# Gated recurrent attention and a PReLU network in one kernel: three edits of a hand-written order

## The chip, the cores and the metric

The kernel runs on one core of a Trainium2 chip. A core has five engines that each work through their own list of instructions in order: TensorE (PE in the profile, with its weight loads as PEld), VectorE (DVE), ScalarE (ACT), GpSimd (POOL) and SyncE (SP), which only issues transfers. ScalarE and POOL issue transfers too. The engines meet through semaphores alone. The metric is the device time of one execution in microseconds (us), lower is better.

## The reference

A recurrence per batch and head (4 batches, 8 heads, 768 steps in time, 48 dimensions), followed by a two-layer network on its output:

```python
f = 1.0 / (1.0 + np.exp(-f_logit))
for t in range(S):
    state = f[:, :, t, :, None] * state + np.einsum('bhd,bhe->bhde', k[:, :, t], v[:, :, t])
    y[:, :, t] = np.einsum('bhd,bhde->bhe', q[:, :, t], state)
x = y.transpose(0, 2, 1, 3).reshape(B * S, H * D)        # 3072 x 384
h = x @ w_in                                             # 384 x 2048
g = np.maximum(h, 0.0) + alpha * np.minimum(h, 0.0)
return g @ w_out                                         # 2048 x 384
```

## The kernel before, in words

Time is cut into 6 chunks of 128, the batches into 2 pairs. A step is one chunk of one pair, so there are 12 steps, and each handles 256 tokens. Inside a chunk the recurrence is unrolled into products of decayed q and k over blocks of 32 and 64, with a state carried from chunk to chunk in the v tile `vs`.

The work of a step is written as four generators, which give control back at every `yield`:

- `prepare` loads f, q, k and v, takes the sigmoid, and builds the decays and the scaled q and k, nearly all on VectorE. Its last part copies `q3` into `A` on ScalarE (L407).
- `carry` multiplies across blocks (`off`, L432 and L442), copies that into `ad` and `A` on ScalarE (L446, L450), in the first chunk also transposes k on TensorE (`pk`) and copies it (`ksn`, L462). A second part makes the state's update (`pd`) and adds it to `vs` (L482 to L488).
- `attend` makes the products inside the blocks of 32 (`raw` L508, `qu` L523), places them under masks on VectorE (L514, then L529 or L545), copies them into `A` (L551), multiplies with `vs` (`py`, L562) and copies the result to `y`. `y` becomes `xT`: in the first step by products with a 0/1 matrix (`xt`, L580), later by small transfers (L591).
- `network` computes the two layers for the step's 256 tokens: `ph` (L606) into a PSUM bank, its negative part on ScalarE (`neg`, L611), the gate on VectorE (L613). In the first step the second layer is the plain product `po` (L626). From the second on it is seven products of half matrices (`pa` to `pe`, L645), which need sums of gates (`S`, L687) and sums of quarters of w_out (t2, t3, t4 and b12, L706).

The weights come as 64-bit floats and are turned into 32-bit ones on the chip, in 8 pieces each for w_in and w_out. A piece is one load on SP's queue (L196) into one of 4 `raw` buffers, three ScalarE activations (L201, L203, L204, some 2.6 us together), and then on VectorE a difference (L214, `lead`) and a 16-bit addition (L219). SP's load of a piece waits until the third activation of the piece four before it has read the buffer. Piece n of w_in serves the n-th `ph` of the first step; piece n of w_out serves two of the 16 row blocks of `po`.

PSUM is shared out in two pools that go round: two pairs of banks (`off`, `pk`, `raw`, `qu`, `pd`, `py`) and four single banks (`xt`, `ph`, `po`, `pa` to `pe`). A product that takes a bank waits until the reader of the tile before has finished with it. So the first `po` takes the bank that the gates of the fifth `ph` free, and in later steps the first `ph` takes the bank of `pb`, which L668 frees.

Nothing plans the order on TensorE, VectorE and ScalarE. It is written out by hand in strings, one per step, and the instructions of these three engines are issued in exactly the order in which the strings call the generators (POOL and SP follow from what the tiles need). Each letter advances one generator to its next `yield`, and a digit repeats it:

- `P` is the step's own `prepare`, `Q` the `prepare` of the step after it, `O` is `carry`, `S` is `attend`, and `n` is `network` of the step before.
- `a` is the ScalarE part of the next w_in piece and its load, `w` the VectorE part: the difference of one piece and the addition of the piece before it. `b` and `v` are the same for w_out.
- `W` advances `halves_of_w_out`: the first call only makes room, then come t3, t2, t4 and b12, each in two VectorE instructions.

The first four steps have strings of their own in `first` (L712 to L717), all others share `usual`.

Of the kernel before, what the change touches and what calls it, by code (L numbers as in the profile page):

```python
# [31 lines left out]
def kernel(  # L32
# [39 lines left out]
    W = U * HP * C  # L72
# [66 lines left out]
    for m in range(1, NB):  # L139
        lo = UO[m] + (4 if m == 1 else 0)  # L140
        n = NB - m
# [4 lines left out]
    for half in range(2):  # L146
        for m in range(1, NQ):
            n = NQ - m
# [540 lines left out]
    def halves_of_w_out():  # L689
# [20 lines left out]

    steps = [(bp, c) for c in range(NC) for bp in range(B // U)]
    first = (  # L712
        "P5 a w P a2 O w S w a w a2 S Q S O S w Q2 S Q2 S w",
        "a2 w b w n O w n b2 v S P v2 n2 S b v Q n b n O S2 v n b v n Q2 b v Q b n S v2 W Q W S n2 W n W",
        "n S P n2 S n W n O Q n3 O S Q n S Q n Q S2 Q n3",
        "S n3 P S Q S n O n O n4 Q S Q S Q n S Q n Q n2",
    )  # L717
    usual = "S n2 S n O n O n Q n3 Q n Q S3 n Q S n Q n Q n"
# [80 lines left out]
```

## Time and profile before

| | us |
|---|---|
| median of 3 runs | 623.29 |
| lowest and highest | 623.14, 623.50 |
| the profiled execution, whole | 625.07 |
| its span, first to last instruction | 623.3 |
| granted TensorE clock over the span | 0.997 |

An instruction row of the profile gives its start, its length (of several merged ones, from first start to last end), engine, line, operation, output and input, shape and count. In square brackets stand the idle time of the engine just before it and what ended it. A row of the chain or of waits names who waited for whom. Times of instructions overlap slightly, because an engine's next instruction starts before the last one has been written out.

The start-up (loads, weights, the first step) reaches to about 105 us, when the second step's first `ph` begins. From about 157 us on the kernel goes round once per step, in equal distances of 47.3 us, until about 534 us; behind that come the rest of the last step and the network of its tokens.

### The profile page before, as it was taken

The page shows a single profiled execution, that of the slowest core. Times are in us where ns is not written, and L with a number is a line of the kernel's source. Part 1 is how long each engine was busy: PE and PEld are TensorE (multiplying, and loading weights), DVE is VectorE, ACT ScalarE, POOL GpSimd, SP SyncE. Part 2 cuts the span into 40 slices and gives each one's busy share as a digit, 9 for nine tenths or more (in the row PEclk, how much of TensorE's full clock was granted, in tenths as well). Part 3 has the DMA queues.
Part 4 walks back from the last instruction along what each step waited for, and adds up shares of the span by engine and source line. Part 5 has one row for each costly group of instructions (what it writes and reads, how often), then busy time and mean ns, then how long its engine had stood idle before and what let it go on. Part 6 is the DMA issues. An engine that isn't in the chain of part 4 may idle for free.

```text
span 623.3 us, 19117 instructions
## 1 busy us (share of the span) xinstructions
PE 589.7 (95%) x8220; PEld 526.0 (84%) x8220; DVE 503.7 (81%) x1013; ACT 260.4 (42%) x482; POOL 62.7 (10%) x119
## 2 busy tenths in 40 slices
PE   3458999999999999999999999999999999999997
PEld 3347866789899899889889889889889889889997
DVE  7589989899799699899889888888888889762261
ACT  5797992270443252352342343343243244223110
POOL 9020010001001001001001001001001000000000
PEclk9999999899999999999999999999999999999999
DMA  9865613213313313313313413313313301201000
GB/s 306 271 226 187 215 40 90 72 35 88 85 36 93 79 35 86 87 35 85 88 35 85 87 36 85 87 35 87 73 49 85 71 19 26 53 3 26 26 1 25
DMA packets 68116, 50.43 MB, mean 81 GB/s; under 512 B 47168, under 2 KB 60608, under 8 KB 68032
## 3 DMA queue, kind: packets, MB, share of 16 engines
q1 hardware_dynamic: 56656, 25.01, 15.6%
q0 software_dynamic: 6864, 22.35, 12.3%
q10 hardware_dynamic: 4512, 1.85, 1.6%
q8 instruction: 65, 1.06, 0.7%
q14 instruction: 19, 0.16, 0.1%
HBM read 36.21 MB, written 4.72 MB: 66 GB/s over the span
## 4 chain that ended last, share of the span: by engine, by line
PE 58%; DVE 15%; ACT 12%; issue 3%; ACTq 0%; DMA 0%; DVEq 0%
PE ph L606 23%; PE pc L645 9%; PE pa L645 6%; PE pe L645 5%; PE pd L645 5%; ACT A L551 4%; DVE gate L613 3%; ACT us L302 3%; DVE S L687 3%; PE qu L523 3%; PE raw L508 2%; DVE qd L275 2%; PE py L562 2%; ACT neg L611 2%; PE pb L645 1%
## 5 line engine op out<-in xcount | busy, mean ns | idle before, releaser
L606 PE MATMUL ph<-xT,w_in_sb 128*128 128x256 f32 x1152 | 262.3, 385 | 0.0
L606 PEld LDWEIGHTS ph<-xT,w_in_sb 128*128 128x128 f32 x1152 | 216.4, 191 | 32.9 <-issue 2.5
L611 ACT ACTIVATE neg<-ph 128x512 f32<-128x512 f32 x96 | 57.2, 597 | 196.5 <-PE ph L606 157.3
L613 DVE SCALAR_TENSOR_TENSOR gate<-neg,om,ph 128x256 f32<-128x256 f32 x192 | 82.1, 477 | 48.9 <-ACT neg L611 48.7
L645 PE MATMUL pc<-t,S 128*128 128x192 f32 x352 | 61.7, 329 | 0.0
L645 PE MATMUL pa<-w_out_sb,gate 128*128 128x192 f32 x352 | 61.0, 327 | 0.0
L645 PEld LDWEIGHTS pa<-w_out_sb,gate 128*128 128x128 f32 x352 | 58.0, 190 | 0.6
L645 PEld LDWEIGHTS pc<-t,S 128*128 128x128 f32 x352 | 57.3, 190 | 0.6
L514 DVE COPY_PREDICATED ad<-mraw,raw 128x256 f32<-128x256 int32 (+1 forms) x96 | 42.4, 442 | 8.3 <-PE raw L508 5.8
L529 DVE COPY_PREDICATED ad<-mquad,qu 128x224 f32<-128x224 int32 (+6 forms) x140 | 42.0, 300 | 6.2
L407 ACT COPY A<-q 48x512 f32<-48x512 f32 x44 | 27.2, 617 | 37.5 <-DVE q L356 37.1
L551 ACT COPY A<-ad 32x256 f32<-32x256 f32 x96 | 38.6, 402 | 1.4
L318 DVE TENSOR_TENSOR us<-us,fs 128x768 f32<-128x768 f32 (+5 forms) x60 | 36.8, 614 | 0.0
L663 ACT COPY o<-pa 128x192 f32<-128x192 f32 x11 | 3.5, 319 | 75.2 <-PE pa L645 72.3
L508 PEld LDWEIGHTS raw<-qd,k 48*32 48x32 f32 x1536 | 18.4, 109 | 16.6 <-issue 8.8
L562 PEld LDWEIGHTS py<-A,vs 128*64 128x64 f32 x768 | 25.7, 145 | 7.8 <-ACT A L551 3.3
L508 PE MATMUL raw<-qd,k 48*32 48x80 f32 x1536 | 23.4, 243 | 9.3 <-ACT A L450 7.0
L562 PE MATMUL py<-A,vs 128*64 128x64 f32 x768 | 28.8, 232 | 3.4 <-ACT vs L488 1.3
L687 DVE TENSOR_TENSOR S<-gate 128x512 f32<-128x512 f32 x44 | 30.3, 688 | 0.8
L645 PE MATMUL pb<-t,gate 128*128 128x192 f32 x176 | 30.4, 326 | 0.0
L645 PE MATMUL pd<-w_out_sb,S 128*128 128x192 f32 x176 | 30.4, 326 | 0.0
L645 PE MATMUL pe<-w_out_sb,S 128*128 128x192 f32 x176 | 30.4, 326 | 0.0
(109 smaller groups left out, 756.0 us busy)
## 6 DMA issues: line engine op xcount, KB each, us to landing
w_out_raw<-in_w_out SPq DMA_DIRECT2D x8, 767.8 KB, 4.2
w_in_raw<-in_w_in SPq DMA_DIRECT2D x8, 767.2 KB, 9.9
q<-in_qT POOLq DMA_DIRECT2D x11, 512.0 KB, 4.1
f<-in_fT POOLq DMA_DIRECT2D x11, 512.0 KB, 4.3
k<-in_kT POOLq DMA_DIRECT2D x11, 512.0 KB, 4.7
out<-o SPq DMA_DIRECT2D x24, 192.0 KB, 2.8
vs<-in_v POOLq DMA_DIRECT2D x22, 192.0 KB, 4.6
ksn<-kt SPq DMA_DIRECT2D x80, 32.0 KB, 2.0
```

Of the source, the lines that this page charges most:

```text
L318: nc.vector.tensor_tensor(us[:, :, UO[m]:UO[m] + 4 * n].rearrange("p g (i r) -> p g i r", r=4), us[:, :, skip:skip + 4 * n].rearrange("p g ...
L407: nc.scalar.copy(A[halves(cc)[1], :, par * HP:(par + 1) * HP, CH * cc:CH * (cc + 1)], q3[rows(par)].rearrange("p (u h c) s t -> p u h c (s ...
L508: nc.tensor.matmul(raw[DB * j:DB * (j + 1), par, hp * C:hp * C + QW], lhsT=k[r_, g * DB:(g + 1) * DB], rhs=qd[r_, g], start=True, stop=True)
L514: nc.vector.copy_predicated(adu[:, :, :, d:4], mraw[:, d, :, d:4].bitcast(I32).unsqueeze(1).broadcast_to((128, H, NB, n)), rv[:, :, QO[d]: ...
L529: nc.vector.copy_predicated(ad[:, u, :, :, 4 * m:DB], mquad[:, lo:lo + n].bitcast(I32).unsqueeze(1).unsqueeze(1).broadcast_to((128, 2, HP, ...
L551: nc.scalar.copy(A[s_, u, :, s_], ad[s_, u].rearrange("p r h t -> p (r h) t"))
L562: nc.tensor.matmul(py[64 * par:64 * par + 64, u, o:o + CH], lhsT=vs[bp][:, cc, u, hd * D:hd * D + 64], rhs=A[:, u, par * HP + hp, CH * cc: ...
L606: nc.tensor.matmul(ph[:, j * T:(j + 1) * T], lhsT=w_in_sb[:, kt, m * 128:(m + 1) * 128], rhs=xT[:, kt], start=(kt == 0 and j == 0), stop=( ...
L611: nc.scalar.activation(neg, phv, AF.Relu, scale=-1.0)
L613: nc.vector.scalar_tensor_tensor(gate[:, m % NH, m // NH], neg[:, j], om[:, m:m + 1], phv[:, j], ALU.mult, ALU.add)
L645: nc.tensor.matmul(to[:, 0:DH], lhsT=of(f), rhs=by(f), start=(f == 0 and not more), stop=(f == NH - 1), skip_group_check=True)
L687: nc.vector.tensor_tensor(to, x_, y_, op)
```

## The change

Three edits in the strings, nothing else:

1. In the first string `a w P a2 O` becomes `a2 w P a O`: the ScalarE part of w_in piece 1 (with its load) comes ahead of the last part of the first `prepare` (the L407 copies) and not behind it. The VectorE order of these letters is the same in both.
2. In the second string `a2 w b w n O w n` becomes `a2 w2 n O b w n`: the ScalarE part of w_out piece 0 goes behind the second step's first `carry` part (L446, L450, L462) and still stands ahead of the second `neg`. The VectorE order of these letters is the same in both.
3. The third of the four differences, t4 (`W`), leaves the end of the second string and comes back in the third, behind the second `S` (behind the second half of `raw`, `qu` and their masked copies), ahead of the fourth gate. b12 stays where it was.

```diff
     first = (
-        "P5 a w P a2 O w S w a w a2 S Q S O S w Q2 S Q2 S w",
-        "a2 w b w n O w n b2 v S P v2 n2 S b v Q n b n O S2 v n b v n Q2 b v Q b n S v2 W Q W S n2 W n W",
-        "n S P n2 S n W n O Q n3 O S Q n S Q n Q S2 Q n3",
+        "P5 a2 w P a O w S w a w a2 S Q S O S w Q2 S Q2 S w",
+        "a2 w2 n O b w n b2 v S P v2 n2 S b v Q n b n O S2 v n b v n Q2 b v Q b n S v2 W Q W S n2 W n",
+        "n S P n2 S W n W n O Q n3 O S Q n S Q n Q S2 Q n3",
         "S n3 P S Q S n O n O n4 Q S Q S Q n S Q n Q n2",
     )
```

## The prediction

> **What bounds the kernel now.** I read the page first, then the chain of waits by time, then each engine in order of time from 12 to 166 us, the only stretch whose order changes.
>
> ```profile
> PE 589.7 (95%) x8220; PEld 526.0 (84%) x8220; DVE 503.7 (81%) x1013; ACT 260.4 (42%) x482; POOL 62.7 (10%) x119
> ```
>
> TensorE (PE) is the bound overall: in the chain, `raw` recurs at 202.99, 250.17, 297.52 and 344.83, a step of 47.3 us that the change leaves alone. So what counts is how much earlier TensorE enters that rhythm. In the first 157 us the bound changes hands. ScalarE (ACT):
>
> ```profile
> 14.57 0.88 ACT L204 ACTIVATE w_in_sb<-w_in_raw 128x768 int32<-128x768 uint32 x1
> 19.81 1.25 ACT L407 COPY A<-q 48x512 f32<-48x512 f32 x2 [4.37 <-DVE q L356]
> 21.07 0.99 ACT L201 ACTIVATE w_in_pos<-w_in_raw,bias 128x768 int16<-128x768 int16 x1
> 23.62 0.97 ACT L201 ACTIVATE w_in_pos<-w_in_raw,bias 128x768 int16<-128x768 int16 x1
> 26.13 0.42 ACT L446 COPY ad<-off 128x128 f32<-128x128 f32 x2
> ...
> 57.03 1.01 ACT L201 ACTIVATE w_out_pos<-w_out_raw,bias 128x768 int16<-128x768 int16 x1
> 59.62 0.60 ACT L611 ACTIVATE neg<-ph 128x512 f32<-128x512 f32 x1
> 61.69 1.07 ACT L462 COPY ksn<-pk 128x512 f32<-128x512 f32 x2
> 62.65 0.61 ACT L611 ACTIVATE neg<-ph 128x512 f32<-128x512 f32 x1
> ```
>
> ScalarE stands 4.37 us before the copies of L407. After them, its waits from 20 to 95 us are those two words below: L407's own, and 4.2 us on the `xt` products. Otherwise it never pauses, so until 95 us any time saved before L446 is saved for everything behind it. From 87.5 to 157 us VectorE (DVE) in turn has a single wait:
>
> ```profile
> ACT A L407 <- DVE q L356: 4.4, 1, 4.4
> ACT xT L582 <- PE xt L580: 4.2, 3, 2.2
> ...
> DVE gate L613 <- ACT neg L611: 0.8, 1, 0.8
> ```
>
> TensorE around the places that move, and VectorE where it hands over:
>
> ```profile
> 61.72 0.92 PE L508 MATMUL raw<-qd,k 48*32 48x80 f32 x64 [1.80 <-ACT A L450]
> 81.90 5.32 PE L626 MATMUL po<-w_out_sb,gate 128*128 128x384 f32 x16
> 114.84 1.01 PE L508 MATMUL raw<-qd,k 48*32 48x80 f32 x64
> 117.21 1.07 PE L523 MATMUL qu<-us,k 48*32 48x112 f32 x64 [1.36 <-DVE ad L529]
> 118.21 7.23 PE L606 MATMUL ph<-xT,w_in_sb 128*128 128x256 f32 x24
> 157.18 8.04 PE L606 MATMUL ph<-xT,w_in_sb 128*128 128x256 f32 x36
> ...
> 108.43 3.56 DVE L706 TENSOR_TENSOR t<-t,w_out_sb 128x768 f32<-128x768 f32 x4
> 156.30 0.35 DVE L668 TENSOR_TENSOR o<-Csum,pb 128x192 f32<-128x192 f32 x1
> ...
> 60.88:64.29 3.41, 2.39 (x131) 2.08 (x132) 2.20 (x5) 3.37 (x8) 0.00 (x0) 1.00 0.64 225
> 115.50:118.91 3.41, 2.04 (x96) 1.48 (x84) 3.24 (x11) 0.09 (x1) 0.73 (x1) 1.00 0.41 84
> 118.91:122.32 3.41, 3.41 (x9) 2.70 (x10) 3.05 (x9) 0.00 (x0) 0.00 (x0) 0.50 0.21 80
> ```
>
> The last three lines are stretches of 3.41 us: length, busy time of TensorE, its weight loads, VectorE, ScalarE and POOL, then the granted TensorE clock, which is 0.50 in the third. The 24 `ph` of 118.21 take 7.23 us where 24 others take 5.45, so the half clock cost 1.78 us.
>
> **Part 1, w_in piece 1 ahead of L407.** Its three activations take 23.62 − 21.07 = 2.55 us and now go into the 4.37 us gap, 15.4 to 18.0, if the piece is there. It is: issued at 4.66, landed 9.9 later, at 14.6.
>
> ```profile
> w_in_raw<-in_w_in SPq DMA_DIRECT2D x1, 767.2 KB, 9.9
> ```
>
> L407 still waits for VectorE until 19.81; piece 2 follows (landed at 16.6: issued 5.33, 11.3 us), L446 starts at 23.6, not 26.13. Its inputs are ready (`off` done 20.6, `pk` 22.5). `raw` waits for L450 and starts 2.55 earlier (27.75), then the predicated copies (29.24), and all three engines shift by 2.55. VectorE's two-operation step for piece 1, which now waits 2.39 us, starts at once.
>
> What else moves with it: SP's load of piece 5 waits for piece 1's last activation and leaves at 18.1 instead of 23.74, behind piece 4 (15.47, 10.0 us to land) and beside POOL's q, f and v loads (issued 14.2 to 17, 5.6 to 8.3 us). It is wanted at 31.2, so even 10 us leaves 3 us; f, landed at 23.2, is wanted at 33.8. POOL's order is unchanged; its waits on these engines move with them. Cost: nothing.
>
> One thing need not move: `xt` starts at half speed (spacing 0.427 us) and reaches 0.216 only from 50.65, 3.8 us in. If that switch came 2.96 us in (the next earlier 3.41 us stretch), 0.43 more is gained; if it missed all 12 products, 0.6 is lost (3 × 0.21). I take zero between these.
>
> **Part 2, O before b.** ScalarE does the same work from 57.03 to 63.2 in another order: `neg0`, L446 to L462, the w_out group, `neg1`. So `neg1` and everything later on ScalarE stay at −2.55. L446 to L462 move another 2.59 (59.62 − 57.03): `raw` could start at 61.72 − 5.14 = 56.6, but `ph1` ends at 57.4, so TensorE gains about 4.4 there. Queued behind the w_out group is `neg1`, and VectorE's gate 1 waits for it as it does now. VectorE is therefore at −2.55 and gates 4 and 5 (79.83, done 81.47) free their banks at 78.92. `po` needs them: TensorE, which could be there at 77.4, starts `po` at 78.9, −2.98. Of its lead over the other two 0.4 is left. SP's w_out piece 4 leaves 0.5 us later than now (buffer of piece 0), wanted 13 us after: nothing.
>
> **Part 3, t4.** It is all that changes place on VectorE. Four `t` instructions take 3.56 us, so t4's two 1.78. Without them gate 0 starts 1.78 earlier still, and L529 ends at 117.07 − 2.55 − 1.78 = 112.74. TensorE's second `raw` ends at 113.2, so `qu` has no 1.36 us wait; with it goes the low stretch ahead of the half clock. t4 returns behind the second L529, where VectorE idled 0.77 for `neg`. That idle is filled too: TensorE's products end at 116.9, VectorE comes at 120.3. t4 is read from 137 on, b12 (1.82 us) by `pd` at 142.8; both are done by 126. No POOL or SP instruction moves.
>
> **Sum.** VectorE: 2.55 + 0.77 = 3.32 earlier through 157. TensorE would be about 5.2 earlier at `raw` (155.50): 2.98 at `po`, 1.36 and 1.78 at `qu` and `ph`, less rests. But the next step's first `ph` needs the bank that L668 frees; it now ends 156.65, 0.53 ahead of `ph`. The shift is 3.32 + 0.53 = 3.85 us. After that TensorE bounds.
>
> The profiled execution took 625.07 us (span 623.3 and 1.77 around it); it would become 621.2. The median of the three shown, 623.29, lies 1.78 below it: 619.4.
>
> [...] The row: after 1.36 us of idle between two groups of small products the clock fell to 0.50. [...]
>
> **Rivals.**
>
> *One half-clock stretch after the change.* TensorE waits about 1.35 us at L668's bank right after `raw` and `qu`, much like 115.5 to 118.9. For: that row. Against: the stretch 60.88 to 64.29 holds 1.0 us of idle and the same small products and the clock stayed at 1.00. Price 1.7: there, where TensorE bounds, 623.29 − 2.15 = 621.1; ahead of `po`, VectorE's slack takes half: about 620.4.
>
> *VectorE does not hold it.* If its chain to L668 shrinks, TensorE's 5.2 comes through: 618.1. For: TensorE's waits vanish. Against: the wait list shows no idle to shrink.
>
> *The first gap is not filled.* If piece 1 landed after 19.8, part 1 gives nothing, and what is left is 0.77 + 0.53 = 1.3: 622.0. Against: 14.6, and even piece 3 landed at 18.6.
>
> *Slower.* The clock again, repeatedly: TensorE, running ahead of its partners from 57 to 157 us, stops at `po`, `qu` and the L668 bank, and each stop brings half-clock stretches of 3.41 us, 1.7 us each on the bound. From three in full, 5.1 against 3.85, it is slower than before, at 624.5. Against: with half speed TensorE no longer runs ahead, so stops end themselves.
>
> **How the numbers follow.** Forecast as summed, 618.8 to 620.2 with `xt`'s bounds: 0.50. One half-clock stretch, 620.4 to 621.1: 0.20. More, near 618.1: 0.10. First gap not filled or gain mostly eaten, 622.0 and up to no change: 0.10. Slower: 0.10. The range leaves out the last two: 618.0 to 621.6. A difference of 0.2%, 1.25 us, is what this measurement can tell from none. The first three cases are beyond it, and part of the fourth: faster 0.83, same 0.07, slower 0.10.
>
> **What would show it.** Right: L407 still at 19.8 with a wait of about 1.7 left, L446 at 23.6; `raw` near 57.3 without a wait; a short wait before `po` near 79; `qu` near 113 without its wait and no half clock after it; VectorE unbroken from 85 to 154; L668 at 153.0 and `ph` at 153.4. Wrong: a DMA wait at 15.4; a clock of 0.50 after 60 us; `xt` much slower; or the 47.3 us step itself changed.

## The result, and the profile after

The changed kernel takes 620.21 us (median of 5 runs, 620.11 to 621.47) where the kernel before takes 623.35 beside it (5 runs, 623.14 to 623.50): a ratio of 0.9951, 95% interval 0.994 to 0.9962. That is 3.1 us faster, and ends 0.8 us above the 619.4 forecast. The profiled execution of the changed kernel is the one of 620.21 us (span 618.4).

The page's line of busy times, which hardly moves:

```profile
PE 587.5 (95%) x8220; PEld 524.4 (85%) x8220; DVE 503.3 (81%) x1013; ACT 260.9 (42%) x482; POOL 63.0 (10%) x119
```

ScalarE in order of time, then its list of waits from 12 to 95 us:

```profile
14.60 0.98 ACT L201 ACTIVATE w_in_pos<-w_in_raw,bias 128x768 int16<-128x768 int16 x1 [0.57 <-DMA w_in_raw<-in_w_in]
19.97 1.25 ACT L407 COPY A<-q 48x512 f32<-48x512 f32 x2 [2.72 <-DVE q L356]
21.25 1.01 ACT L201 ACTIVATE w_in_pos<-w_in_raw,bias 128x768 int16<-128x768 int16 x1
23.80 0.40 ACT L446 COPY ad<-off 128x128 f32<-128x128 f32 x2
...
55.88 1.07 ACT L462 COPY ksn<-pk 128x512 f32<-128x512 f32 x2 [0.66 <-PE pk L459]
```

```profile
ACT A L407 <- DVE q L356: 2.7, 1, 2.7
ACT xT L582 <- PE xt L580: 2.3, 3, 1.3
ACT ksn L462 <- PE pk L459: 0.7, 1, 0.7
ACT w_in_pos L201 <- DMA w_in_raw<-in_w_in: 0.6, 1, 0.6
```

Piece 1 now runs at 14.60, L407 has not moved (19.97), one piece and not two stands between it and L446, and L446 begins at 23.80 where it began at 26.13. The third row of the waits is new: L462 now comes before its `pk` is ready. TensorE and VectorE where the prediction named a time:

```profile
44.68 2.83 PE L580 MATMUL xt<-y,dense 128*128 128x256 f32 x12 [1.69 <-ACT y L571]
53.82 1.97 PE L459 MATMUL pk<-ident,ks 128*128 128x128 f32 x8 [0.30 <-DVE vs L486]
58.92 0.92 PE L508 MATMUL raw<-qd,k 48*32 48x80 f32 x64
78.69 5.32 PE L626 MATMUL po<-w_out_sb,gate 128*128 128x384 f32 x16
112.40 1.07 PE L523 MATMUL qu<-us,k 48*32 48x112 f32 x64
152.23 8.04 PE L606 MATMUL ph<-xT,w_in_sb 128*128 128x256 f32 x36 [0.74 <-DVE Csum L667]
...
85.11 0.76 DVE L305 TENSOR_TENSOR_SCAN ps<-fs,ones 128x289 f32<-128x289 f32 x1
117.87 1.82 DVE L706 TENSOR_TENSOR t<-t,w_out_sb 128x768 f32<-128x768 f32 x2
151.83 0.35 DVE L667 TENSOR_TENSOR Csum<-pc,Csum 128x192 f32<-128x192 f32 x1
152.21 0.35 DVE L668 TENSOR_TENSOR o<-Csum,pb 128x192 f32<-128x192 f32 x1
```

The 1.36 us wait ahead of `qu` is gone, as is the half clock behind it (the granted clock is 1.00 from 56.9 us to the end of the span), and t4 stands at 117.87. From 84 to 157 us VectorE waits for nothing. The last step of the lead is the wait at 152.23: `ph` starts 0.05 us after L667 ends (152.18). Its bank is therefore freed by L667, which reads `pc`, and not by L668, as the text ahead of the result had it.

Two rows serve as yardsticks below: the third start of L305 (VectorE begins the third preparation; in the change, in part 1 alone and in both pairs no wait holds VectorE up from there to the third network) and the `ph` that begins the third network, after which the kernel goes on in its even rhythm of 47.3 us. In the profiled pair L305 moves from 88.24 to 85.11 (−3.13) and `ph` from 157.18 to 152.23 (−4.95). The pair shows more than the medians do, because this execution of the kernel before was one of 625.07 us and held the half clock (0.50 from 118.92 to 122.33 us).

### The profile page after: what moved, and what is told of

The parts are those of the page before. It is cut to its first block, busy times and chain, and to the rows that moved or that the text cites. A ratio compares the mean times of both kernels' runs of the same rounds, so it can differ in the third digit from the quotient of the medians.

```text
span 618.4 us, 19117 instructions
## 1 busy us (share of the span) xinstructions
PE 587.5 (95%) x8220; PEld 524.4 (85%) x8220; DVE 503.3 (81%) x1013; ACT 260.9 (42%) x482; POOL 63.0 (10%) x119
## 3 DMA queue, kind: packets, MB, share of 16 engines
q10 hardware_dynamic: 4512, 1.85, 1.7%
HBM read 36.21 MB, written 4.72 MB: 66 GB/s over the span
## 4 chain that ended last, share of the span: by engine, by line
PE 54%; DVE 24%; ACT 15%; issue 4%; DMA 2%; SPq 0%; ACTq 0%; DVEq 0%
PE ph L606 21%; PE pc L645 9%; PE pa L645 6%; PE pd L645 5%; ACT A L551 4%; DVE gate L613 4%; PE pe L645 4%; ACT us L302 3%; DVE S L687 3%; DVE qd L275 3%; PE raw L508 3%; PE qu L523 3%; PE py L562 2%; ACT neg L611 2%; DVE vs L482 1%
## 5 line engine op out<-in xcount | busy, mean ns | idle before, releaser
L645 PEld LDWEIGHTS pc<-t,S 128*128 128x128 f32 x352 | 57.3, 190 | 0.6
L514 DVE COPY_PREDICATED ad<-mraw,raw 128x256 f32<-128x256 int32 (+1 forms) x96 | 42.4, 441 | 9.5 <-PE raw L508 7.0
L407 ACT COPY A<-q 48x512 f32<-48x512 f32 x44 | 27.2, 619 | 35.9 <-DVE q L356 35.5
L645 PEld LDWEIGHTS pe<-w_out_sb,S 128*128 128x128 f32 x176 | 28.9, 190 | 0.0
```

The lines of the kernel that those rows point to most:

```text
L407: nc.scalar.copy(A[halves(cc)[1], :, par * HP:(par + 1) * HP, CH * cc:CH * (cc + 1)], q3[rows(par)].rearrange("p (u h c) s t -> p u h c (s ...
L514: nc.vector.copy_predicated(adu[:, :, :, d:4], mraw[:, d, :, d:4].bitcast(I32).unsqueeze(1).broadcast_to((128, H, NB, n)), rv[:, :, QO[d]: ...
L645: nc.tensor.matmul(to[:, 0:DH], lhsT=of(f), rhs=by(f), start=(f == 0 and not more), stop=(f == NH - 1), skip_group_check=True)
```

## The experiments

Three theories were set against each other. A: the time is what ScalarE hands to VectorE at 84 to 88 us, so that part 1 is nearly all of it. B: the prediction's sum, in which part 3 gives 0.77 us on VectorE and 0.53 more at the bank. C: the lead that part 2 gives TensorE counts.

| kernel | median us (before beside it) | ratio, 95% | `xt` us | third L305 | L667 ends | `ph` | L305 to `ph` |
|---|---|---|---|---|---|---|---|
| before | 623.35 | | 4.72 | 88.24 | 156.27 | 157.18 | 68.94 |
| the change | 620.21 (623.35) | 0.9951, 0.9940 to 0.9962 | 2.83 | 85.11 | 152.18 | 152.23 | 67.12 |
| the change again | 621.05 (623.49) | 0.9960, 0.9947 to 0.9972 | 5.46 | 86.96 | 154.03 | 154.09 | 67.13 |
| part 1 alone | 621.61 (624.15) | 0.9953, 0.9941 to 0.9965 | 2.83 | 85.34 | 152.40 | 152.89 | 67.55 |
| part 2 alone | 624.02 (624.15) | 0.9997, 0.9988 to 1.0006 | 4.26 | 87.93 | 155.85 | 156.80 | 68.87 |
| part 3 alone | 623.36 (624.15) | 0.9986, 0.9978 to 0.9995 | 2.83 | 87.99 | 155.07 | 155.12 | 67.13 |
| parts 1 and 2 | 622.35 (624.15) | 0.9966, 0.9951 to 0.9980 | 2.83 | 84.89 | 151.92 | 152.40 | 67.51 |
| parts 1 and 3 | 621.20 (623.49) | 0.9960, 0.9948 to 0.9973 | 4.31 | 85.46 | 152.54 | 152.60 | 67.14 |
| wait of `qu` filled | 624.26 (623.49) | 1.0015, 1.0006 to 1.0024 | 2.83 | 87.69 | 154.81 | 155.74 | 68.05 |
| piece 2 ahead too | 620.62 (623.49) | 0.9961, 0.9947 to 0.9974 | 4.21 | 85.47 | 152.52 | 152.57 | 67.10 |
| the same, 13 products fewer | 623.26 (623.41) | 0.9995, 0.9981 to 1.0009 | 2.83 | 86.12 | 153.19 | 153.25 | 67.13 |
| clock kept up | 620.00 (623.41) | 0.9944, 0.9932 to 0.9956 | 2.86 | 85.02 | 152.08 | 152.13 | 67.11 |
| t4 on GpSimd | 620.06 (623.41) | 0.9943, 0.9929 to 0.9958 | 4.23 | 85.83 | 151.16 | 151.84 | 66.01 |
| both of these | 618.89 (623.68) | 0.9928, 0.9915 to 0.9940 | 2.86 | 84.53 | 149.90 | 150.18 | 65.65 |

The last five columns are of one profiled execution each; the one of before is that of 625.07 us. Where a kernel has added lines, the same instructions stand a few lines further down (L667 as L671 or L675, `xt` at L588, `ph` at L610 or L614).

### Each part alone, and in pairs

Part 1 alone:

```diff
-        "P5 a w P a2 O w S w a w a2 S Q S O S w Q2 S Q2 S w",
+        "P5 a2 w P a O w S w a w a2 S Q S O S w Q2 S Q2 S w",
```

> Part 1 by itself: w_in piece 1 ahead of the L407 copies, w_out piece 0 and t4 where they were. Theory A (ScalarE alone: what counts is the moment at which ScalarE releases VectorE for its unbroken stretch at 84 to 87 us, so parts 2 and 3 only shuffle work inside engines): 2.5 to 3.3 us faster than before, 620.0 to 620.8. Theory B (the prediction's sum: part 1 brings 2.55, t4 another 0.77 and the bank's slack): about 2.6 faster or less, but at least 0.7 slower than the whole change. Theory C (TensorE's lead from part 2 is what pays): under 1 us faster.

Part 2 alone:

```diff
-        "a2 w b w n O w n b2 v S P v2 n2 S b v Q n b n O S2 v n b v n Q2 b v Q b n S v2 W Q W S n2 W n W",
+        "a2 w2 n O b w n b2 v S P v2 n2 S b v Q n b n O S2 v n b v n Q2 b v Q b n S v2 W Q W S n2 W n W",
```

> Part 2 by itself: the second step's first carry ahead of w_out piece 0 on ScalarE. Theory A: no difference, 623.0 to 623.7, because the second neg and all that follows on ScalarE stay where they are; raw starts about 2 to 2.6 us earlier at 59 to 60 us and then waits again before po. Theory B: the same. Theory C: 1.5 to 3 us faster, 620.3 to 621.8.

Part 3 alone:

```diff
-        "a2 w b w n O w n b2 v S P v2 n2 S b v Q n b n O S2 v n b v n Q2 b v Q b n S v2 W Q W S n2 W n W",
-        "n S P n2 S n W n O Q n3 O S Q n S Q n Q S2 Q n3",
+        "a2 w b w n O w n b2 v S P v2 n2 S b v Q n b n O S2 v n b v n Q2 b v Q b n S v2 W Q W S n2 W n",
+        "n S P n2 S W n W n O Q n3 O S Q n S Q n Q S2 Q n3",
```

> Part 3 by itself: t4 behind the second half of the masked copies. Theory A: no difference in time, 623.0 to 623.7, in runs in which TensorE's clock does not fall near 118 us, because VectorE's chain up to L667 near 156 us holds the same instructions without a gap; qu near 115.9 instead of 117.2. Theory B: 0.77 of VectorE's idle time and the bank's slack of 0.53 to 0.9 are gained, 1.3 to 1.7 us, so 621.6 to 622.0.

Parts 1 and 2 together (t4 at its old place), and parts 1 and 3 together (the second string as before but for its last `W`):

```diff
+        "P5 a2 w P a O w S w a w a2 S Q S O S w Q2 S Q2 S w",
+        "a2 w2 n O b w n b2 v S P v2 n2 S b v Q n b n O S2 v n b v n Q2 b v Q b n S v2 W Q W S n2 W n W",
...
+        "P5 a2 w P a O w S w a w a2 S Q S O S w Q2 S Q2 S w",
+        "a2 w b w n O w n b2 v S P v2 n2 S b v Q n b n O S2 v n b v n Q2 b v Q b n S v2 W Q W S n2 W n",
+        "n S P n2 S W n W n O Q n3 O S Q n S Q n Q S2 Q n3",
```

> The change without part 3, t4 at its old place. Theory A: as fast as the whole change, 620.0 to 621.0, with L667 near 152.2 and qu again waiting for L529 near 113. Theory B: 0.8 to 1.3 us slower than the whole change, 621.0 to 621.5.

> Parts 1 and 3 without part 2 (the w_out group stays ahead of the second step's first carry). Theory A: the same time as the whole change within 0.4 us, raw near 59 to 61 us behind a wait. Theory C (TensorE's lead from part 2 pays): at least 1.5 us slower than the whole change.

Part 1 alone has a ratio of 0.9953, the whole change 0.9951 and 0.9960: part 1 is nearly all of it, as theory A has it. Part 2 is not to be told from nothing alone (0.9997), and without it nothing is lost (0.9960 against 0.9960). Theory C falls. Part 3 alone is 0.8 us faster than before, clear of noise: more than the nothing of theory A, less than the 1.3 to 1.7 of theory B. Parts 1 and 2 missed both forecasts, A's 620.0 to 621.0 and B's 621.0 to 621.5: three of the eight runs took 620.4 to 620.5 us, five 622.0 to 623.4. The profile is of the fastest of them, so what the five others lost stays open; the interval (0.9951 to 0.9980) overlaps that of part 1 alone.

The last column of the table sorts itself into three groups, and tells what part 3 does. With t4 at its new place L305 to `ph` takes 67.10 to 67.14 us in all seven profiles (t4 on GpSimd set aside). With t4 at its old place it takes 67.51 and 67.55. With t4 at its old place and a half clock behind `qu` it takes 68.87 and 68.94. (The kernel with the wait of `qu` filled, below, stands apart.) So moving t4 buys 0.4 us, and 1.4 us more where it avoids the half clock. How the 0.4 comes about is seen in the timeline of part 1 alone:

```profile
114.32 1.07 PE L523 MATMUL qu<-us,k 48*32 48x112 f32 x64 [1.20 <-DVE ad L529]
152.89 7.39 PE L606 MATMUL ph<-xT,w_in_sb 128*128 128x256 f32 x33
...
85.34 0.75 DVE L305 TENSOR_TENSOR_SCAN ps<-fs,ones 128x289 f32<-128x289 f32 x1
152.05 0.35 DVE L667 TENSOR_TENSOR Csum<-pc,Csum 128x192 f32<-128x192 f32 x1
```

The 1.20 us wait at `qu` sets TensorE back so far that it reaches `ph` 0.49 us after the bank has been freed (152.40). In the changed kernel it comes too early and waits 0.74. VectorE itself gains nothing from t4's new place: from the third L305 to the fourth it takes 51.32 us in part 1 alone (85.34 to 136.66) and 51.33 in the change (85.11 to 136.44). In the kernel before it takes 52.30, and 52.19 in part 2 alone: the idle time in front of a gate, which the prediction wanted to fill with t4, stands only where the half clock makes `ph` late. Part 2 alone shows that stretch too (columns as in the prediction; the half clock is the 0.50):

```profile
114.54:117.95 3.41, 2.16 (x130) 1.73 (x129) 3.20 (x11) 0.60 (x1) 0.73 (x1) 1.00 0.28 29
117.95:121.36 3.41, 3.41 (x10) 2.78 (x9) 3.14 (x8) 0.00 (x0) 0.00 (x0) 0.50 0.33 135
```

The wait at `qu` alone does not bring the half clock: in part 1 alone and in parts 1 and 2 TensorE waits there for 1.2 us too, and the clock stays at 1.00 from 57 us to the end of the kernel (the mean over the span is 0.997 in both, which one stretch of 3.41 us at 0.50, ahead of 57 us, accounts for). What decides between the two was not found.

### The wait of `qu` filled, in the kernel before

Three dense products are put into the second `raw` tile before its own, so that TensorE is busy where it would wait for VectorE; the real products overwrite them.

```diff
             raw = pair(f"raw{u}_{i}")
+            if (bp, c, u) == (0, 1, 1):
+                for _ in range(3):
+                    nc.tensor.matmul(raw[:, 0, 0:256], lhsT=w_in_sb[:, 0, 0:128],
+                                     rhs=w_in_sb[:, 0, 0:256], start=True, stop=True)
```

> The kernel before, with three dense 128x128x256 products (1.3 us of TensorE's work, overwritten at once) ahead of the raw products whose successor qu waits 1.36 us for L529 near 117 us. The wait stays, but TensorE is busy through it. If the wait as such costs the time that part 3 gains: as before, 624.0 to 624.4. If the half clock that follows it in some runs costs it: no run above 624.4, median 623.3 to 623.7, as with part 3 alone, and no half clock near 118 us.

In its profile the 24 `ph` behind `qu` take 5.45 us and not 7.23, so the half clock stayed away, and L305 to `ph` takes 68.05 instead of 68.94. It is still 0.5 us more than in part 1 alone, and the runs are slower by 0.15%; four of the eleven lie above 625 us, which the second theory excluded. The filling costs more than the half clock does on average, so it tells no more of the size of the latter: inconclusive.

### The change again

The changed kernel beside parts 1 and 3, on another chip than each part alone.

> The whole change once more, beside the others, because single runs of every kernel differ by up to 2 us with the stretches in which TensorE's clock is at half. Theory A (time lies where ScalarE releases VectorE; t4 counts only where it keeps the clock up): 620.1 to 621.5, 3 to 3.5 us under the median of before. Theory B (prediction's sum): 3.85 under it, 620.3 where before has 624.15.

The gain is 2.44 us here and 3.14 in the first series. The two profiled executions (620.21 and 621.96 us) differ first at `xt`:

```profile
44.67 5.46 PE L580 MATMUL xt<-y,dense 128*128 128x256 f32 x12 [1.69 <-ACT y L571]
```

At `y` the two profiles of the same kernel still agree to 0.01 us (43.46 and 43.45). Then the twelve products take 2.83 us in the one and 5.46 in the other, and the third L305 follows at 85.11 and 86.96. The granted clock changed to 1.00 at 43.2 us in the one and at 50.9 in the other.

### Piece 2 ahead as well

```diff
-        "P5 a2 w P a O w S w a w a2 S Q S O S w Q2 S Q2 S w",
+        "P5 a3 w P O w S w a w a2 S Q S O S w Q2 S Q2 S w",
```

> The change with w_in piece 2 too ahead of the L407 copies. In the changed kernel ScalarE still stands 2.72 us before them, and the piece has landed by about 16.7. Theory A and B: ScalarE is another 2.5 us earlier at L446 (near 21.2), and all of it reaches the end: 617.5 to 618.9. Rival: something other than ScalarE binds next in the first step (the pk transposes end near 22.5, piece 4 lands near 25.4): under 1 us faster than the change.

620.62 us, not to be told from the change (621.05 beside it; the two intervals lie upon each other). ScalarE does come to L446 2.3 us earlier than in the change, at 21.53, but TensorE cannot use it. Its timeline, VectorE's wait behind it, and ScalarE's behind that:

```profile
23.16 1.01 PE L508 MATMUL raw<-qd,k 48*32 48x80 f32 x38 [0.61 <-ACT A L450]
26.93 0.63 PE L508 MATMUL raw<-qd,k 48*32 48x80 f32 x21 [2.75 <-issue]
...
27.83 1.88 DVE L514 COPY_PREDICATED ad<-mraw,raw 128x256 f32<-128x256 int32 x4 [5.81 <-PE raw L508]
30.72 0.55 DVE L214 TENSOR_TENSOR w_in_lead<-w_in_pos,w_in_neg 128x768 bf16<-128x768 bf16 x1
...
31.35 1.03 ACT L201 ACTIVATE w_in_pos<-w_in_raw,bias 128x768 int16<-128x768 int16 x1 [1.95 <-issue]
```

TensorE stands 2.75 us in the middle of `raw`, waiting for nothing that the profile shows. In that stretch the trace has a transfer of 16,384 bytes of the kind "instruction", from 24.44 to 25.56. In the change the same place costs 1.11 us: the transfer runs from 24.46 to 25.65 there too, but `raw` begins only at 25.42. L514 then begins at 27.83 here and at 28.13 in the change, so 0.30 is left of 2.3. ScalarE loses its lead with it: `w_in_pos` has three buffers, and L201 needs the one that VectorE's L214, in order behind L514, has to read first. L201 begins 0.08 us after that L214 ends (31.27) here, after 1.95 us of idle time, and 0.08 us after it in the change too (31.58 and 31.66), where ScalarE paused for only 0.07. So the change already stands where ScalarE can gain no more without an earlier L514. `y` follows at 43.17, 0.29 earlier than in the change.

### The same with 13 products fewer

```diff
-IDLE = 56
+IDLE = 43
```

> The changed kernel with both remaining pieces of the first network weights' activations before the copies of ScalarE (as in the run before it, which was no better than the change: 620.6 us), and 13 of the 56 tiny products at the start of TensorE's program left out, so that every later instruction of TensorE lies 26 places further ahead. Theory of instruction supply: the 2.75 us that TensorE stood idle between the 38th and the 39th product of the first `raw` came from the place at which its instruction stream crosses into the next block; with the border moved to the end of that `raw`, VectorE's first conditional copy starts at 24.4 to 25.5 us instead of 27.8, `y` at or below 42 us instead of 43.2, and the time is 618.5 to 619.8 us. Rival (the idle time has another cause, or the lead is lost again at `pd` and `py`): `y` at 43.0 to 43.5 us and 620.2 to 621.0 us.

Worse, and not as expected: 623.26 us, with runs from 621.20 to 625.52. The stop did not go to the end of `raw`; it went to the middle of `off`:

```profile
19.28 0.93 PE L442 MATMUL off<-us 48*32 48x16 f32 x73 [0.55 <-DVE us L392]
23.73 0.76 PE L442 MATMUL off<-us 48*32 48x16 f32 x55 [3.52 <-issue]
```

Again there is one such transfer within the stop, from 21.24 to 22.29, and TensorE goes on 1.44 us after its end (1.37 in the run above). The transfer that the kernel before has at 10.50 us and the change at 10.60, where TensorE waits 9.26 and 9.42 us for VectorE's `q` anyway, is missing. So the theory's place was wrong, while its cause is supported: with nothing but the tiny products ahead changed, the stop is at another place, and again with a transfer in it. What sets off a transfer, and when, was not settled. Nor does the stop explain the whole loss: the profile is of the fastest of the twelve runs, with `y` at 44.44, 1.27 us later than with all 56 products, while by the two ratios the median is some 2.1 us higher; the rest stays open.

### The clock kept up for `xt`

Four dense products into a bank that nothing reads, in the first step only: two behind the first four of `py`, two behind all of them.

```diff
+    def filler(n):
+        for _ in range(n):
+            nc.tensor.matmul(idle[:, 0:224], lhsT=ident, rhs=dense[:, 0:224], start=True, stop=True)
...
                                          start=True, stop=True)
+                    if not (bp or c) and (u, hp, cc) == (0, 0, 0):
+                        filler(2)
+        if not (bp or c):
+            filler(2)
         yield
```

> The changed kernel with four dense 128x128x224 products into an unused bank in the first step: two behind the first product pairs of `py`, two between `py` and `xt`. Clock theory: part of the spread from run to run (620.1 to 622.1 us) is the clock that `xt` finds, 2.83 us in one profile of the change and 5.46 us in the other; with TensorE kept busy through the two waits (1.34 and 1.69 us) before it, `xt` takes at most 3.3 us in the profile, the runs lie within 620.0 to 621.0 us, and the median falls by 0.3 to 0.8 us beside the change. Rival (the filling does not reach the gate's grid, or delays `xt`): `xt` still takes 4 us or more or starts 0.6 to 1.3 us later, and the median is 620.6 to 622.0 us.

The median is 620.00 us and all five runs lie within 619.72 to 620.26; those of the change reach from 620.11 to 621.96 over its two series. In the profile:

```profile
38.29 1.86 PE L496 MATMUL idle<-dense,ident 128*128 128x224 f32 x4
42.43 1.02 PE L496 MATMUL idle<-dense,ident 128*128 128x224 f32 x4
44.78 2.86 PE L588 MATMUL xt<-y,dense 128*128 128x256 f32 x12 [1.33 <-ACT y L579]
```

`xt` takes 2.86 us, as in the profiles with the clock up ahead of it (2.83), and starts only 0.10 us later than in the change. The rival, that the filling misses the clock's stretches or delays `xt`, falls. The gain of the median over the change is within the noise (0.9944 against 0.9951 and 0.9960); what the runs show is the smaller spread. (The profile counts a dense product as two, so two of them are "x4".)

### t4 on GpSimd

```diff
-                nc.vector.tensor_tensor(to[:, p], x_[:, p], y_[:, p], op)
+                (nc.gpsimd if to is t4 else nc.vector).tensor_tensor(to[:, p], x_[:, p], y_[:, p], op)
```

> The changed kernel with the matrix difference t4 computed on GpSimd instead of VectorE. Theory that VectorE's last unbroken stretch (84 to 152 us) sets the end, but only by the 0.74 us that `ph` waits for L667: L667 ends near 150.4 us instead of 152.2, the wait of `ph` vanishes, `ph` starts at 151.5 us, and the time falls by 0.5 to 0.8 us to 619.4 to 619.8 us. Prediction's sum taken literally (VectorE's whole 1.78 us counts): 618.4 us. Rival (GpSimd's traffic slows VectorE's instructions beside it, or another wait takes its place): 620.2 us or more, with L667 not before 151.8 us.

The timeline of GpSimd, VectorE and TensorE:

```profile
107.06 4.24 POOL L706 TENSOR_TENSOR t<-t,w_out_sb 128x768 f32<-128x768 f32 x2 [12.68 <-DMA ksn<-kt]
...
85.83 0.75 DVE L305 TENSOR_TENSOR_SCAN ps<-fs,ones 128x289 f32<-128x289 f32 x1
150.81 0.35 DVE L667 TENSOR_TENSOR Csum<-pc,Csum 128x192 f32<-128x192 f32 x1
...
151.84 8.04 PE L606 MATMUL ph<-xT,w_in_sb 128*128 128x256 f32 x36
```

This profile had a slow `xt` (4.23 us), so its times are read from L305 on: L667 ends 65.33 us behind it where the change takes 67.07, 1.74 less, t4's whole time. `ph` has no wait and comes 1.11 us earlier (66.01 against 67.12), held by TensorE itself now. That is more than the 0.74 of the wait, less than the 1.74 of VectorE: the prediction's sum taken literally falls. The median is 620.06 us, between what the theory (619.4 to 619.8) and its rival (620.2 or more) named, with runs from 618.81 to 621.59; its gain over the change is within the noise.

### Both

The edits of the last two kernels in one.

> Both of the last two edits in one kernel: the four dense products that kept the clock up for `xt` (alone 620.0 us, five runs within 0.54 us), and the matrix difference t4 on GpSimd (alone 620.06 us, runs from 618.81 to 621.59 us). If the two act on separate things, as the theory says (the one removes the runs in which `xt` takes 4 to 5.5 us, the other the 0.74 us that `ph` waits for L667), their gains add up: `xt` 2.8 to 3.3 us, no wait of `ph`, all runs within 618.8 to 619.8 us, median 619.3 us, ratio to the kernel before 0.9935. Rival (an earlier TensorE only meets another release): median 619.8 us or more, with a wait of 0.5 us or more at `po`, `pa` or `ph` between 84 and 157 us.

618.89 us, ratio 0.9928 (0.9915 to 0.9940). The interval touches that of the change in its first series (from 0.9940) and lies below that of the second (from 0.9947); five of the six runs are below every run of the change, which makes it very likely faster. TensorE's timeline, and all that its list of waits holds from 80 to 160 us:

```profile
44.89 2.86 PE L588 MATMUL xt<-y,dense 128*128 128x256 f32 x12 [0.99 <-ACT y L579]
150.18 5.01 PE L614 MATMUL ph<-xT,w_in_sb 128*128 128x256 f32 x22
```

```profile
PE qu L527 <- DVE vs L486: 0.3, 1, 0.3
```

The medians agree with two gains that add up, and the rival's new wait does not appear. Five runs lie within 618.52 to 619.47; one, at 620.74, does not, and its cause stays open.

## Why the prediction was right, point by point

**Part 1: right in mechanism and size.** Piece 1 was there in time (it kept ScalarE 0.57 us, which the 4.37 us gap covers), L407 stood still, L446 was forecast at 23.6 and came at 23.80. At equal length of `xt` (2.83) the third L305 of part 1 alone comes 2.35 us before that of the filled `qu` and 2.65 before that of part 3 alone, whose orders are that of before up to there; the prediction had 2.55. The first masked copies (L514) moved by only 1.12 (29.24 to 28.13) and not by 2.55, because of the stop of 1.11 us in `raw`; ScalarE lost only 0.07 us by that, so `y` still moved by 2.14.

**Part 2: right that it brings nothing in the end, wrong in its stations.** `raw` was to start near 57.3 and started at 58.92. Ahead of it stood a stop of 1.23 us in `off`, for nothing that the profile shows, and a half-clock stretch, in which `pk` took 1.97 us (1.09 in parts 1 and 3, which had none there):

```profile
53.48:56.89 3.41, 3.11 (x16) 2.80 (x13) 3.38 (x6) 2.66 (x10) 0.00 (x0) 0.50 0.92 309
```

L462 now waits 0.66 for that `pk`; with part 2 undone the group of b covers it. `po` came at 78.69 (78.9 forecast), 78.95 without part 2. By 152 us nothing is left of it.

**Part 3: this step failed.** "That idle is filled too", worth 0.77 us on VectorE, was wrong: the idle time belonged to the half clock in the one execution that was profiled. VectorE's way from L305 to L305 is the same with t4 moved or not (51.33 and 51.32), and the filled `qu`, with t4 at its old place and no half clock there, has no such idle time either. Part 3 does remove the wait at `qu` and what followed from it, which is worth 0.4 us, or 1.8 in an execution with the half clock.

**The bank: wrong row, nearly right size.** The bank is freed by L667. Its slack ahead of `ph` was 0.91 us in the profile of before, and 0.49 in part 1 alone, which has no half clock there; the prediction took 0.53 at L668.

**The sum.** The prediction subtracted 3.85 us from the profiled execution, and then 1.78 for the distance to the median. But 0.77 of the 3.85 was to be had only in an execution with the half clock, which the 1.78 had taken out already. No execution near the median of before was profiled, but the distances say that it holds no half clock at `qu`: the earliest third L305 without part 1 (87.69), 68.87 to `ph` with the half clock and at least 467.87 from `ph` to the end (the least in any profile) make 624.4 us, an estimate, and the median is 623.35. Without the 0.77 the same sum is 3.08, and 623.29 − 3.08 = 620.2; 620.21 was measured. That they meet to 0.01 us is luck: the second series of the same kernel gained 2.44 and not 3.14. In the profiled pair itself the shift at `ph` was 4.95, not 3.85: 3.13 before L305 and 1.82 behind it, of which the half clock is 1.4 and the move of t4 0.4.

**`xt`: bounds too narrow.** The prediction let it gain 0.43 or lose 0.6 beside 4.72 us. The profiles show 2.83 to 5.46, −1.89 to +0.74. The step that failed is the place of the clock's stretches: the prediction kept them where the one profile of before had them, and counted one stretch of 3.41 us earlier at most. In the profiles the rise ahead of `xt` or in it lies anywhere from 41.1 to 50.9 us. The forecast survived because much of that is given back. In all six profiles with an `xt` of 2.83 (the change, parts 1 and 3 each alone, parts 1 and 2, the filled `qu`, the 13 products fewer) the clock is up from 43 to 46 us and drops again, 10.2 us after it rose, for 3.4 us; in those with an `xt` of 4.2 to 5.5 it rises later (at 50.65 in before and at 50.9 in the change again), or dips inside `xt`, and there is no such drop at 53 to 58. Part 3 alone had the 2.83 and the drop from 55.0 to 58.5, and its third L305 came at 87.99, no sooner than the 87.93 of part 2 alone with 4.26.

**The rivals.** "VectorE does not hold it" named 618.1 as TensorE's own time; with t4 off VectorE and the clock kept up, runs reach 618.5. "One half-clock stretch" after `raw` at 155 did not come: no profile of a kernel with t4 at its new place shows a lowered clock between 60 and 600 us (1.00 throughout in the change), though TensorE waits 0.74 us at that bank. The one at 53.5 is another place. "The first gap is not filled" and the slower case did not occur.

## What to carry to other kernels

Before a gap seen in one profiled execution is counted as a gain, see whether a low clock made it, and whether the execution that gives the median has that low clock at all: here 0.77 us was subtracted twice. Where engines hand the lead to each other, take one row behind the last hand-over as a yardstick, and compare distances from it between kernels; here that separated 0.4 us from a spread of 2 us. Here four dense products in TensorE's waits bought steadier times (619.72 to 620.26 us against 620.11 to 621.96), being together no longer than the waits (1.86 and 1.02 us against 1.34 and 1.69); the kernel with the wait of `qu` filled, where they were longer than the wait (1.53 against 1.36 us), was slower (624.26 against 623.49).

## What the runs showed that was not expected

- The same program finds another clock from run to run. In the profile of before the granted clock falls to 0.50 at 118.92 us and is back at 1.00 at 122.33; in that of the change it is 0.50 from 26.18 to 43.24 and from 53.48 to 56.90. Those three stretches are 3.41, 17.06 and 3.42 us long; the long one is five of the short ones to within 0.05 us. The rise ahead of `xt` or in it comes at 43.2 us in one profile of the change and at 50.9 in the other, which is 2.63 us in `xt` and 1.85 at L305.
- TensorE stood for 2.75 us (piece 2 ahead) and 3.52 us (the same with 13 products fewer) early in the kernel, each time with an instruction transfer of 16,384 bytes in the stop; that the transfer made the stop is the author's reading. The one ate the gain of moving piece 2; the other came when 13 tiny products were left out, which is part of why the ratio went from 0.9961 to 0.9995.
- GpSimd's two differences of 128x768 took 4.24 us together where VectorE's take 1.82, and VectorE was not slowed beside them: it gained 1.74 us, which is just the distance from t4 to the next instruction in the change (117.87 to 119.61).
